# Dropping the row norms of queries and keys, and moving the low-part subtraction of the attention weights from GpSimd to VectorE

## The chip, the cores and the metric

The kernel runs on one core of one Trainium2 chip. The metric is the time of one execution in device microseconds. Before the change three runs gave 878.05, 881.35 and 883.31 us; their median, 881.35 us, is the time before.

## The reference

Inputs: q, k, v of 2 batches x 8 heads x 768 tokens x 64; 16 centroids of 64 for each head; two feed-forward layers of 512 -> 2048 -> 512, whose weights come as float64; and alpha (2048).

```
q_n = q / (norm(q) + 1e-6);  k_n, c_n likewise
q_assign = argmax over clusters of q_n . c_n;  k_assign likewise
scores = where(q_assign == k_assign, q k^T / 8, -1e9)
attn = softmax(scores);  x = attn v           # 1536 tokens x 512
h = x w1_in;  x = (h * sigmoid(h)) w1_out
h = x w2_in;  x = (max(h,0) + alpha * min(h,0)) w2_out
```

A token's own norm scales all 16 of its similarities by the same positive factor. The position of the largest one does not depend on it (ties by rounding apart).

## The kernel before

Every float32 operand of a matrix product is scaled by a power of two and split into two fp16 parts, high and low; three products (high-high, high-low, low-high) are summed in PSUM. The split of something takes two steps: a copy to fp16 (the high part) and a subtraction that leaves the low part.

A **unit** is one head of one tile of 128 tokens; there are 12 tiles x 8 heads = 96 units. For a unit, `front` issues:

- on TensorE the scores, 128 x 768, in two banks of PSUM (L482 the cluster mask, L486 the product itself);
- on VectorE the largest score of a row (L498, over 768), then the scale (L501) and the bias (L502) of the exponential, one number a row each;
- on ScalarE the exponential (L504) and its fp16 copy, the high part (L511);
- the subtraction that makes the low part (L513), on VectorE for the 12 units that `P_LO_DVE` names and on GpSimd for the other 84;
- on SyncE's queue the transposing DMA of both parts (L519), from one of two buffers `hl` that the units use in turn.

Two units later `back` multiplies the transposed weights with the values (L531). `attention` is a generator over the units. Between them it prepares keys and values of a head pair (`prep_k_0`, `prep_k_a`, `prep_k_b`, `prep_v`) and the queries of the next tile (`prep_q_a`, `prep_q_b`). These find each row's cluster: `one_hot` scales the similarities by the inverse row norm (L276), finds the largest (L277), compares (L278) and so on. The inverse norms come from `reduce_sum` over the squares (L335 for keys, L435 for queries) and from `inv_norm`: a power on GpSimd (L296; at the start a square root on ScalarE, L294), an add (L297) and a reciprocal (L298), both on VectorE.

The weights come in pieces of 1 MB. A piece is turned from float64 to float32 by `to_f32` (ScalarE L596 and L600, or GpSimd L604 for the scaling; VectorE L607 and L610 put the bits together) and split by `split` (GpSimd L617 and VectorE L618, or other mixes). The first layer runs in seven chunks of one or two tiles (`layer1`: L858 and L889 on TensorE, L864 and L868 on ScalarE, L865 and L869 on VectorE), with the units dealt out between its steps (`UNITS_BY_CHUNK`). The second layer (L961, L992) follows, with its own weights prepared before and beside it.

What stands here is the order of issue in the program. The framework's scheduler then sets the order on each engine, from its own model of times. Each engine takes its instructions in that order; semaphores between the engines are set by the framework. GpSimd and VectorE work beside each other. A buffer's next writer waits for its last reader.

Of the kernel before, what the change touches and what calls it, by code (L numbers as in the profile page):

```python
# [9 lines left out]
F32 = mybir.dt.float32  # L10
# [4 lines left out]
ACTF = mybir.ActivationFunctionType  # L15
# [3 lines left out]
# Token tiles per chunk of the first layer: (first, number).  # L19
CHUNKS = ((0, 1), (1, 1), (2, 2), (4, 2), (6, 2), (8, 2), (10, 2))  # L20
# The order of issue. A unit is one head of one token tile; "by chunk" says how far the
# units are to be issued by the end of a chunk of the first layer.
# [11 lines left out]
# Which engine does what: "a" ScalarE, "p" GpSimd (by batch and head pair, or by weight and  # L34
# piece; SPLIT has the modes of split()); the units whose low parts VectorE makes.
# [4 lines left out]
P_LO_DVE = (33, 35, 37, 39, 57, 59, 61, 63, 65, 67, 69, 71)  # L40
# [6 lines left out]
def cluster_attention_silu_prelu(  # L47
# [13 lines left out]
    """Cluster-masked attention, then a SiLU and a PReLU feed-forward layer.  # L61

    Every float32 operand of a product is scaled by a power of two (found on the
    chip from a norm, so that nothing overflows) and split into fp16 parts
    hi + lo; hi*hi + hi*lo + lo*hi accumulate in float32.
    Token 6p+t of a batch sits on partition p of tile t.
    """
    nc = tc.nc
# [88 lines left out]
    def pow2_scale(ss_ps, n, top, smax, s_out, inv_out):  # L157
        """s = 2^e with sqrt(ss) * s <= 2^top (and s <= 2^smax); inv = 1/s."""
        u = scr(n).bitcast(I32)
        nc.vector.tensor_scalar(u, ss_ps.bitcast(I32), 24, None, op0=ALU.logical_shift_right)  # L160
        if smax is not None:
            nc.vector.tensor_scalar(u, u, float(max(0, 62 + top - smax)), None, op0=ALU.max)
        e = 189 + top
        nc.vector.tensor_scalar(
            s_out.bitcast(I32), u, float(-e), -BIT23, op0=ALU.add, op1=ALU.mult
        )
        nc.vector.tensor_scalar(
            inv_out.bitcast(I32), u, float(254 - e), BIT23, op0=ALU.add, op1=ALU.mult
        )
# [13 lines left out]
    def psum(kind, *dims):  # L183
        """A bank of PSUM: of the scores', of preparations, of weight norms and layers, or
        (once the preparations are over) any of the last two for layers."""
# [20 lines left out]
    def all_sum(cols, kind="m"):  # L206
        """Sum over partitions (and over the given [128, n] groups), on every partition."""
        n = cols[0].shape[1]
        ps = psum(kind, n)
        for i, c in enumerate(cols):  # L210
            nc.tensor.matmul(out=ps, lhsT=ones, rhs=c, start=(i == 0), stop=(i == len(cols) - 1))
        return ps

    def bc(a, n):
        return a.unsqueeze(2).to_broadcast([128, a.shape[1], n])

    def issue_after(later, earlier):
        """Keep two instructions of one engine in order."""
# [51 lines left out]
    def one_hot(sims, rn, n, w2, o, a, b):  # L270
        """w2[:, :, 64:80] = a * (cluster is the first of the highest sims) + b."""
        x = view(o, F32, n, C)
# [3 lines left out]
        nc.vector.tensor_tensor(out=x, in0=sims, in1=bc(rn, C), op=ALU.mult)  # L276
        nc.vector.reduce_max(out=m, in_=x, axis=AX.X)  # L277
        nc.vector.tensor_tensor(out=y, in0=x, in1=bc(m, C), op=ALU.is_equal)  # L278
# [8 lines left out]
    rn_cols = {H: col(2 * H), 2 * T: col(NP * 2 * T)}  # L287

    def inv_norm(ss, n, early=False):
        """1 / (sqrt(ss) + 1e-6)"""  # L290
        r = rn_cols[n]
        r = r[:, n * ring(f"rn{n}", r.shape[1] // n):][:, :n]
        if early:
            nc.scalar.activation(out=r, in_=ss, func=ACTF.Sqrt)  # L294
        else:
            nc.gpsimd.tensor_tensor(out=r, in0=ss, in1=half[:, 0:n], op=ALU.pow)  # L296
        nc.vector.tensor_scalar(r, r, 1e-6, None, op0=ALU.add)  # L297
        nc.vector.reciprocal(out=r, in_=r)  # L298
        return r

# [20 lines left out]
    def scaled(raw, ss, top, smax, inv, eng, kind):  # L321
        """raw *= s, the power of two that brings the norm under 2^top."""
# [7 lines left out]
    def prep_k_0(b, pr):  # L330
        kr = view(kv_raw(b, pr)[0], F32, G, D)
        sq = view(k_pre(b, pr), F32, G, D)
        ssk, ss = scr(G), scr(1)
        nc.scalar.activation(out=sq, in_=kr, func=ACTF.Square, accum_out=ss)
        nc.vector.reduce_sum(out=ssk, in_=sq, axis=AX.X)  # L335
# [6 lines left out]
        kv_state[b, pr] = inv_norm(ssk, G, b == 0)  # L342
# [42 lines left out]
    def v_scales(b):  # L385
        """No row of the attention output has a larger norm than sqrt(8 m), where m is the
        largest sum of squares of a pair's values in one partition."""
# [8 lines left out]
    def prep_k_b(b, pr):  # L396
        rn = kv_state.pop((b, pr))
# [11 lines left out]
        one_hot(sims, rn, G, w2, k_pre(b, pr), -MASK, 0.0)  # L409
# [14 lines left out]
    q_state = {}  # L424

    def prep_q_a(n):
        raw = view(o_qraw, F32, H, 2, D)[:, :, n % 2, :]
        sq = view(o_preq, F32, H, D)
        ssq = scr(H)
# [5 lines left out]
        nc.vector.reduce_sum(out=ssq, in_=sq, axis=AX.X)  # L435
# [10 lines left out]
        q_state[n] = inv_norm(ssq, H, n == 0)  # L446

    def prep_q_b(n):
        rn = q_state.pop(n)
# [9 lines left out]
        one_hot(sims, rn, H, w2, o_preq, -MASK, MASK)  # L459
# [12 lines left out]
    def front(u):  # L472
# [29 lines left out]
        nc.vector.tensor_tensor(out=bias, in0=nm, in1=scl, op=ALU.mult)  # L502
# [41 lines left out]
    def x_done(n):  # L544
        """Normalise the tile's attention output, split it and transpose the parts."""
# [23 lines left out]
    # float64 bits come in as pairs of 32-bit words. A piece is 1024 elements per partition:  # L569
    # 256 columns of w_in, or two row tiles of w_out.  # L570
# [19 lines left out]
    def to_f32(raw, out, meng):  # L590
        """float64 to float32 by bits: sign, low 8 bits of the exponent's excess over
        2^-127, 20 + 3 bits of the mantissa. The scale by 2^-112 drops the exponent's
        excess range (what lies below 2^-119 stays below it); the last 3 bits come from
        the low word, rounded without a carry (and exactly where float32 is exact)."""
# [43 lines left out]
    def in_tasks(w, raws, o_dst, kind, modes, mp):  # L638
        """Tasks that convert, scale (per piece) and split w_in; and its scales."""
# [41 lines left out]
    def out_tasks(w, raws, o_ts, o_dst, m_in, kind, modes, mp):  # L681
        """The same for w_out: one scale, that also evens out the scales of w_in's pieces."""
# [60 lines left out]
    def attention():  # L743
# [26 lines left out]
        nc.scalar.activation(out=scr(1), in_=kv_state[0, NP - 1][:, 0:1], func=ACTF.Exp)  # L770
# [10 lines left out]
        for u in range(NU + LAG):  # L781
# [11 lines left out]
            # key / value preparation  # L793
# [22 lines left out]
            # query preparation of the next tile  # L816
# [273 lines left out]
```

## Time and profile before

| what | value |
|---|---|
| runs, us | 878.05, 881.35, 883.31 (median 881.35) |
| span of the profiled execution, us | 887.3 (the only time shown of it) |
| TensorE matmul busy | 712.1 us, 80% of the span |
| VectorE (DVE) busy | 627.4 us, 71% |
| ScalarE (ACT) busy | 468.4 us, 53% |
| GpSimd (POOL) busy | 319.1 us, 36% |
| granted TensorE clock, mean | 0.922 |

The shares are averages over very different stages. Up to about 22 us the first loads and preparations run. Up to about 200 us the first layer's weights are prepared beside the first 28 units. Up to about 520 us the other 68 units run, dealt out between the steps of the first layer. Then come the rest of the first layer, the second layer's weights, and from 618 us the second layer itself.

### The profile page before, as it was taken

The page shows a single profiled execution, that of the slowest core. Times are in us where ns is not written, and L with a number is a line of the kernel's source. Part 1 is how long each engine was busy: PE and PEld are TensorE (multiplying, and loading weights), DVE is VectorE, ACT ScalarE, POOL GpSimd, SP SyncE. Part 2 cuts the span into 40 slices and gives each one's busy share as a digit, 9 for nine tenths or more (in the row PEclk, how much of TensorE's full clock was granted, in tenths as well). Part 3 has the DMA queues.
Part 4 walks back from the last instruction along what each step waited for, and adds up shares of the span by engine and source line. Part 5 has one row for each costly group of instructions (what it writes and reads, how often), then busy time and mean ns, then how long its engine had stood idle before and what let it go on. Part 6 is the DMA issues. An engine that isn't in the chain of part 4 may idle for free.

```text
span 887.3 us, 16339 instructions
## 1 busy us (share of the span) xinstructions
PE 712.1 (80%) x6484; PEld 492.5 (56%) x6484; DVE 627.4 (71%) x1298; ACT 468.4 (53%) x866; POOL 319.1 (36%) x216
## 2 busy tenths in 40 slices
PE   1444376766898887789988988879968999999998
PEld 1222255656776776578766767768433444444443
DVE  7999998987869777865986589596895048306700
ACT  7845577736678564565765676878461013102200
POOL 4757764694434652231354432332191000000000
PEclk9995566789899998989999999999998999999999
DMA  8979788657798677486778694455100000000000
GB/s 245 247 204 223 208 221 172 108 120 120 128 153 143 123 150 123 70 145 120 113 108 140 109 242 137 143 189 192 48 1 4 32 13 1 13 24 12 1 24 24
DMA packets 241596, 101.86 MB, mean 115 GB/s; under 512 B 217328, under 2 KB 227568, under 8 KB 241392
## 3 DMA queue, kind: packets, MB, share of 16 engines
q1 hardware_dynamic: 241520, 100.83, 52.8%
q8 instruction: 50, 0.82, 0.4%
q14 instruction: 26, 0.21, 0.1%
HBM read 44.08 MB, written 3.15 MB: 53 GB/s over the span
## 4 chain that ended last, share of the span: by engine, by line
PE 34%; DVE 25%; DMA 17%; POOL 10%; ACT 8%; issue 6%; SPq 1%; POOLq 0%; ACTq 0%; DVEq 0%
DMA arena<-arena 12%; PE w L992 9%; PE w L961 6%; PE m L992 5%; PE m L961 4%; POOL arena L513 4%; PE w L858 4%; DVE arena L607 3%; DMA arena<-in_moe_w_out_dram 2%; DVE arena L869 2%; DVE stat L498 2%; DVE arena L610 2%; PE w L889 2%; ACT arena L511 2%; PE x L531 2%
## 5 line engine op out<-in xcount | busy, mean ns | idle before, releaser
L513 POOL TENSOR_TENSOR arena<-arena 128x768 f16<-128x768 f32 x84 | 147.5, 1763 | 186.7 <-ACT arena L511 184.4
L858 PE MATMUL w<-arena 128*128 128x256 f16 (+1 forms) x1212 | 142.6, 276 | 30.2 <-DVE arena L865 27.7
L858 PEld LDWEIGHTS <-arena 128*128 128x128 f16 x1344 | 127.1, 107 | 56.0 <-issue 37.7
L889 PEld LDWEIGHTS <-arena 128*128 128x128 f16 x1344 | 121.1, 102 | 19.0 <-issue 2.5
L889 PE MATMUL w<-arena 128*128 128x256 f16 (+1 forms) x1200 | 126.1, 264 | 3.2 <-DVE arena L618 1.2
L504 ACT ACTIVATE arena<-s,stat 128x768 f32<-128x768 f32 x96 | 94.5, 985 | 57.0 <-DVE stat L502 42.5
L498 DVE TENSOR_REDUCE stat<-s 128x1 f32<-128x768 f32 x96 | 91.0, 950 | 39.4 <-PE s L486 39.0
L961 PEld LDWEIGHTS <-arena 128*128 128x128 f16 x576 | 57.1, 100 | 80.3 <-issue 15.9
L531 PE MATMUL x<-arena 128*128 128x64 f16 x1728 | 74.9, 203 | 32.0 <-DMA arena<-arena 31.9
L482 PE MATMUL s<-arena 80*128 80x384 f16 x192 | 71.2, 371 | 35.8 <-ACT arena L504 29.7
L511 ACT ACTIVATE arena<-arena 128x768 f16<-128x768 f32 x96 | 80.1, 840 | 32.3 <-DMA arena<-arena 32.2
L992 PEld LDWEIGHTS <-arena 128*128 128x128 f16 x576 | 56.4, 98 | 67.9
L531 PEld LDWEIGHTS <-arena 128*128 128x128 f16 x1728 | 68.9, 105 | 44.6 <-DMA arena<-arena 39.8
L961 PE MATMUL w<-arena 128*128 128x512 f16 x384 | 87.6, 383 | 5.8 <-DVE arena L971 5.8
L992 PE MATMUL w<-arena 128*128 128x512 f16 x384 | 83.9, 379 | 0.0
L974 ACT ACTIVATE arena<-arena,stat 128x512 f16<-128x512 f32 x48 | 34.5, 720 | 88.2 <-DVE arena L971 86.2
L486 PE MATMUL s<-arena 128*128 128x384 f16 x192 | 71.7, 374 | 0.0
L869 DVE SCALAR_TENSOR_TENSOR arena<-arena 128x256 f16<-128x256 f32 (+1 forms) x112 | 62.4, 564 | 5.9 <-ACT arena L868 5.8
L604 POOL TENSOR_SCALAR arena<-arena 128x1024 f32<-128x1024 f32 x28 | 40.6, 1452 | 57.8 <-DMA arena<-in_moe_w_out_dram 32.5
L607 DVE SCALAR_TENSOR_TENSOR arena<-arena 128x1024 int32<-128x1024 int32 x32 | 45.1, 1408 | 20.3 <-ACT arena L600 10.7
L864 ACT ACTIVATE arena<-w,stat 128x256 f32<-128x256 f32 (+1 forms) x101 | 43.3, 432 | 27.9 <-PE w L858 19.4
L970 DVE TENSOR_SCALAR arena<-w,stat 128x512 f32<-128x512 f32 x32 | 23.9, 748 | 46.9 <-PE w L961 46.5
(145 smaller groups left out, 1133.9 us busy)
## 6 DMA issues: line engine op xcount, KB each, us to landing
arena<-in_moe_w_in_dram SPq DMA_DIRECT2D x16, 1024.0 KB, 6.3
arena<-in_moe_w_out_dram SPq DMA_DIRECT2D x16, 1024.0 KB, 5.4
arena<-in_k_dram SPq DMA_DIRECT2D x8, 384.0 KB, 4.3
arena<-in_q_dram SPq DMA_DIRECT2D x6, 512.0 KB, 5.3
arena<-in_v_dram SPq DMA_DIRECT2D x8, 384.0 KB, 5.5
out_dram<-arena SPq DMA_DIRECT2D x12, 256.0 KB, 2.0
arena<-arena SPq DMA_TRANSPOSE x149, 4.0
arena<-in_moe_alpha_dram SPq DMA_DIRECT2D x1, 1024.0 KB, 6.5
```

Of the source, the lines that this page charges most:

```text
L486: nc.tensor.matmul(out=sc[:, j, :hs], lhsT=qt1[:, h], rhs=kt1[:, h % 2, j * hs:(j + 1) * hs], start=False, stop=True,)
L498: nc.vector.tensor_reduce(out=nm, in_=sc[:, :, :hs], axis=AX.XY, op=ALU.max, negate=True)
L504: nc.scalar.activation(out=view(o, F32, 2, hs), in_=sc[:, :, :hs], func=ACTF.Exp, scale=scl, bias=bias, accum_out=sums[n % 2][:, h:h + 1],)
L511: nc.scalar.activation(out=hl[:, 0], in_=p, func=ACTF.Copy)
L513: en.tensor_tensor(out=hl[:, 1], in0=p, in1=hl[:, 0], op=ALU.subtract)
L531: nc.tensor.matmul(out=x_ps[0][:, h], lhsT=pt[:, ph * T + t], rhs=vt[:, h % 2, t, vh], start=(i == 0), stop=(i == 3 * T - 1),)
L607: nc.vector.scalar_tensor_tensor(out=lo, in0=hi, scalar=3, in1=lo, op0=ALU.logical_shift_left, op1=ALU.bitwise_or)
L858: nc.tensor.matmul(out=hp, lhsT=wi[:, a, kd, f % 2 * 128:f % 2 * 128 + 128], rhs=mov(bb, kd), start=(i == 0), stop=(i == 3 * KD - 1),)
L869: nc.vector.scalar_tensor_tensor(out=g[:, f, 1], in0=th, scalar=2.0 ** -16, in1=g[:, f, 0], op0=ALU.mult, op1=ALU.subtract,)
L889: nc.tensor.matmul(out=acc, lhsT=wo[:, a, f % 2, dt * 128:(dt + 1) * 128], rhs=g[:, f, bb], start=(i == 0), stop=(i == 3 * KF - 1),)
L961: nc.tensor.matmul(out=hp, lhsT=in_piece(o_a + 24 * KB, f // 2)[:, a, kd, f % 2 * 128:][:, :128], rhs=x[bb][:, kd], start=(i == 0), stop=( ...
L992: nc.tensor.matmul(out=acc, lhsT=g[:, f, a, t * 128:(t + 1) * 128], rhs=out_piece(o_w, f // 2)[:, bb, f % 2], start=(i == 0), stop=(i == 3 ...
```

## The change

Three edits, besides comments:

1. The row norms go. `inv_norm` and the sums over squares for it are no longer there; `one_hot` looks for the largest similarity in PSUM directly, without the multiplication by the inverse norm. The sum of squares of the whole operand, from which the power of two is found, stays.
2. The bias of the exponential (L502) is made by `tensor_scalar` with one number a row as scalar, in place of `tensor_tensor`.
3. `P_LO_DVE` names all 96 units: each low-part subtraction of the attention weights (L513) is on VectorE.

```diff
-P_LO_DVE = (33, 35, 37, 39, 57, 59, 61, 63, 65, 67, 69, 71)
+P_LO_DVE = range(96)
...
-    def one_hot(sims, rn, n, w2, o, a, b):
+    def one_hot(sims, n, w2, o, a, b):
-        x = view(o, F32, n, C)
         y = view(o + KB, F16, n, C)
         z = view(o, F16, n, C)
         m = scr(n)
-        nc.vector.tensor_tensor(out=x, in0=sims, in1=bc(rn, C), op=ALU.mult)
-        nc.vector.reduce_max(out=m, in_=x, axis=AX.X)
-        nc.vector.tensor_tensor(out=y, in0=x, in1=bc(m, C), op=ALU.is_equal)
+        nc.vector.reduce_max(out=m, in_=sims, axis=AX.X)
+        nc.vector.tensor_tensor(out=y, in0=sims, in1=bc(m, C), op=ALU.is_equal)
...
-    def inv_norm(ss, n, early=False):
-        """1 / (sqrt(ss) + 1e-6)"""
-        r = rn_cols[n]
-        r = r[:, n * ring(f"rn{n}", r.shape[1] // n):][:, :n]
-        if early:
-            nc.scalar.activation(out=r, in_=ss, func=ACTF.Sqrt)
-        else:
-            nc.gpsimd.tensor_tensor(out=r, in0=ss, in1=half[:, 0:n], op=ALU.pow)
-        nc.vector.tensor_scalar(r, r, 1e-6, None, op0=ALU.add)
-        nc.vector.reciprocal(out=r, in_=r)
-        return r
...
-        nc.vector.reduce_sum(out=ssk, in_=sq, axis=AX.X)
...
-        kv_state[b, pr] = inv_norm(ssk, G, b == 0)
...
-        nc.vector.reduce_sum(out=ssq, in_=sq, axis=AX.X)
...
-        q_state[n] = inv_norm(ssq, H, n == 0)
...
-        nc.vector.tensor_tensor(out=bias, in0=nm, in1=scl, op=ALU.mult)
+        nc.vector.tensor_scalar(bias, nm, scl, None, op0=ALU.mult)
...
-        nc.scalar.activation(out=scr(1), in_=kv_state[0, NP - 1][:, 0:1], func=ACTF.Exp)
+        nc.scalar.activation(out=scr(1), in_=isk[0][:, NP - 1:NP], func=ACTF.Exp)
```

The program is shorter, so the line numbers of the changed kernel are smaller: L498, L501, L502 and L513 are L474, L477, L478 and L489 there; L604 and L617 are L580 and L593; L380 is L363; L607, L610 and L618 are L583, L586 and L594.

On **GpSimd**, while the first layer's weights are prepared, subtractions of units (L513) and powers of the norms (L296) stand between the conversions (L604) and splits (L617) of weights before the change:

```order
L380 TENSOR_TENSOR arena<-arena 128x12x64
L513 TENSOR_TENSOR arena<-arena 128x768 x2
L617 TENSOR_SCALAR arena<-arena,stat 128x1024
L604 TENSOR_SCALAR arena<-arena 128x1024
L617 TENSOR_SCALAR arena<-arena,stat 128x1024
L513 TENSOR_TENSOR arena<-arena 128x768 x2
L604 TENSOR_SCALAR arena<-arena 128x1024 x2
L617 TENSOR_SCALAR arena<-arena,stat 128x1024
L513 TENSOR_TENSOR arena<-arena 128x768 x2
L296 TENSOR_TENSOR stat<-stat,half 128x8
```

The same place of GpSimd in the changed kernel, after the low parts of the values (L363):

```order
L363 TENSOR_TENSOR arena<-arena 128x12x64
L593 TENSOR_SCALAR arena<-arena,stat 128x1024
L580 TENSOR_SCALAR arena<-arena 128x1024
L593 TENSOR_SCALAR arena<-arena,stat 128x1024
L580 TENSOR_SCALAR arena<-arena 128x1024 x2
L593 TENSOR_SCALAR arena<-arena,stat 128x1024
```

The weights' instructions keep their order among themselves, and nothing of a unit stands between them.

On **VectorE** near the last units of the attention, before the change, the maximum (L498), scale (L501) and bias (L502) of a unit stand close together, with the last steps of a tile (L557, L560, L561) between them (s with a number is a unit's scores):

```order
L498 TENSOR_REDUCE stat_75<-s_5999 128x1
L557 TENSOR_TENSOR arena_73<-x_5522,stat_75 128x512
L501 TENSOR_SCALAR stat_75<-stat_75 128x1
L498 TENSOR_REDUCE stat_75<-s_6041 128x1
L560 CAST arena_73<-arena_73 128x512
L502 TENSOR_TENSOR stat_75<-stat_75 128x1
```

There, after the change, the subtraction of one unit (L489) stands between the scale (L477) and the bias (L478) of the next:

```order
L474 TENSOR_REDUCE stat_75<-s_5942 128x1
L477 TENSOR_SCALAR stat_75<-stat_75 128x1
L489 TENSOR_TENSOR arena_73<-arena_73 128x768
L478 TENSOR_SCALAR stat_75<-stat_75 128x1
L474 TENSOR_REDUCE stat_75<-s_6008 128x1
```

VectorE now reaches the bias of a unit only past the subtraction of the unit before it. While the weights are prepared, VectorE's order after the change has pieces of weights (L583, L586) and the norm-free steps of `one_hot` (L283, L284) between the bias of a unit (the first L478) and the next subtraction:

```order
L478 TENSOR_SCALAR stat<-stat 128x1
L283 TENSOR_TENSOR arena<-arena,stat 128x128
L583 SCALAR_TENSOR_TENSOR arena<-arena 128x1024
L586 SCALAR_TENSOR_TENSOR arena<-arena 128x1024
L478 TENSOR_SCALAR stat<-stat 128x1
L284 TENSOR_SCALAR arena<-arena 128x8x16
L160 TENSOR_SCALAR stat<-w 128x1
L586 SCALAR_TENSOR_TENSOR arena<-arena 128x1024
L489 TENSOR_TENSOR arena<-arena 128x768
```

Other work thus stands between what ScalarE needs from VectorE for a unit and what VectorE needs back from it.

## Rows read from the trace of the kernel before

**Rows 1.** Busy time of each engine by stage (the columns are named first).
```profile
core 0: us, PE busy (x) PEld busy (x) DVE busy (x) ACT busy (x) POOL busy (x), PEclk, DMA share, GB/s
22.00:200.00 178.00, 96.69 (x1090) 75.59 (x1091) 169.26 (x343) 111.23 (x201) 120.11 (x72) 0.76 0.80 187
200.00:520.00 320.00, 271.58 (x3406) 224.59 (x3403) 240.65 (x599) 201.94 (x409) 130.39 (x80) 0.95 0.75 127
```

**Rows 2.** Groups of VectorE, 22 to 200 us: count | busy us, mean ns | idle before.
```profile
L607 DVE SCALAR_TENSOR_TENSOR arena<-arena 128x1024 int32<-128x1024 int32 x15 | 23.5, 1569 | 0.9 <-POOL arena L604 0.6 <-ACT arena L596 0.3
L610 DVE SCALAR_TENSOR_TENSOR arena<-arena 128x1024 int32<-128x1024 int32 x15 | 22.9, 1534 | 0.0
L618 DVE SCALAR_TENSOR_TENSOR arena<-arena,stat 128x1024 f16<-128x1024 f32 x14 | 22.8, 1631 | 0.0
L502 DVE TENSOR_TENSOR stat<-stat 128x1 f32<-128x1 f32 x27 | 12.4, 461 | 0.0
...
L297 DVE TENSOR_SCALAR stat<-stat 128x8 f32<-128x8 f32 (+1 forms) x6 | 3.4, 564 | 0.7 <-POOL stat L296 0.5
L435 DVE TENSOR_REDUCE stat<-arena 128x8 f32<-128x512 f32 x5 | 3.4, 674 | 0.0
...
L335 DVE TENSOR_REDUCE stat<-arena 128x12 f32<-128x768 f32 x3 | 2.8, 927 | 0.0
...
L276 DVE TENSOR_TENSOR arena<-m,stat 128x128 f32<-128x128 f32 (+1 forms) x8 | 2.4, 301 | 0.0
```

**Rows 3.** Groups of GpSimd, 22 to 200 us.
```profile
L513 POOL TENSOR_TENSOR arena<-arena 128x768 f16<-128x768 f32 x25 | 47.7, 1914 | 24.9 <-ACT arena L511 23.6 <-issue 1.3
...
L296 POOL TENSOR_TENSOR stat<-stat,half 128x8 f32<-128x8 f32 (+1 forms) x7 | 13.8, 1978 | 1.9 <-DVE stat L435 1.8 <-DVE stat L160 0.2
```

**Rows 4.** VectorE by line, whole span: shortest/median/longest ns, first and last start.
```profile
L502 DVE TENSOR_TENSOR stat<-stat x96: 101/153/1652, 39.8 to 522.7; 128x1 f32<-128x1 f32 x96
L501 DVE TENSOR_SCALAR stat<-stat x96: 196/203/215, 37.2 to 522.5; 128x1 f32<-128x1 f32 x96
L513 DVE TENSOR_TENSOR arena<-arena x12: 943/958/1372, 241.0 to 435.7; 128x768 f16<-128x768 f32 x12
L607 DVE SCALAR_TENSOR_TENSOR arena<-arena x32: 1161/1225/2653, 14.6 to 633.9; 128x1024 int32<-128x1024 int32 x32
L610 DVE SCALAR_TENSOR_TENSOR arena<-arena x32: 1207/1216/2661, 16.6 to 636.4; 128x1024 int32<-128x1024 int32 x32
L618 DVE SCALAR_TENSOR_TENSOR arena<-arena,stat x20: 1269/1523/2816, 27.0 to 650.8; 128x1024 f16<-128x1024 f32 x20
L869 DVE SCALAR_TENSOR_TENSOR arena<-arena x112: 273/414/1862, 123.8 to 601.2; 128x256 f16<-128x256 f32 x80, 128x128 f16<-128x128 f32 x32
L551 DVE TENSOR_SCALAR stat<-stat x12: 156/172/2609, 86.9 to 528.6; 128x8 f32<-128x8 f32 x12
```

**Rows 5.** Timeline, two instructions at 464.8 us: start, duration, engine, line.
```profile
464.80 1.64 POOL L513 TENSOR_TENSOR arena<-arena 128x768 f16<-128x768 f32 x1 [2.38 <-ACT arena L511]
...
464.90 1.56 DVE L502 TENSOR_TENSOR stat<-stat 128x1 f32<-128x1 f32 x1
```

**Rows 6.** Groups of VectorE, 200 to 520 us, and of GpSimd last.
```profile
L869 DVE SCALAR_TENSOR_TENSOR arena<-arena 128x256 f16<-128x256 f32 (+1 forms) x70 | 40.1, 580 | 2.8 <-ACT arena L868 2.7
...
L502 DVE TENSOR_TENSOR stat<-stat 128x1 f32<-128x1 f32 x67 | 24.7, 370 | 0.8
...
L513 DVE TENSOR_TENSOR arena<-arena 128x768 f16<-128x768 f32 x12 | 12.2, 1019 | 8.3 <-ACT arena L511 8.2
...
L513 POOL TENSOR_TENSOR arena<-arena 128x768 f16<-128x768 f32 x58 | 97.9, 1696 | 157.0 <-ACT arena L511 156.0 <-POOL arena L326 0.5 <-POOL arena L513 0.2
```

**Rows 7.** Shares of the chain that ended last, 200 to 520 us, by line.
```profile
by line: DMA arena<-arena 27.6%; PE w L858 7.9%; PE w L889 5.7%; POOL arena L513 5.6%; issue 4.8%; DVE stat L498 4.1%; DVE arena L869 4.0%; ACT arena L511 3.9%; PE x L531 3.4%; PE s L486 2.3%; PE s L482 2.3%; DVE arena L865 2.0%; DMA arena<
```

**Rows 8.** Pieces of that chain at 302 us: start, length, what.
```profile
302.17 1.66 POOL stat L296
...
303.85 1.60 DVE stat L297
```

More of the change, by code (lines that the diff above doesn't have):

```diff
@@ L285, in one_hot @@
         nc.vector.tensor_scalar(w2[:, :, D:D + C], y, a, b, op0=ALU.mult, op1=ALU.add)
-    rn_cols = {H: col(2 * H), 2 * T: col(NP * 2 * T)}
-    def inv_norm(ss, n, early=False):
-        r = rn_cols[n]
-        r = r[:, n * ring(f"rn{n}", r.shape[1] // n):][:, :n]
-        if early:
-            nc.scalar.activation(out=r, in_=ss, func=ACTF.Sqrt)
-        else:
-            nc.gpsimd.tensor_tensor(out=r, in0=ss, in1=half[:, 0:n], op=ALU.pow)
-        nc.vector.tensor_scalar(r, r, 1e-6, None, op0=ALU.add)
-        nc.vector.reciprocal(out=r, in_=r)
-        return r
     G = 2 * T
@@ L332, in prep_k_0 @@
         sq = view(k_pre(b, pr), F32, G, D)
-        ssk, ss = scr(G), scr(1)
+        ss = scr(1)
         nc.scalar.activation(out=sq, in_=kr, func=ACTF.Square, accum_out=ss)
-        nc.vector.reduce_sum(out=ssk, in_=sq, axis=AX.X)
         if b == 0 and pr == 0:
@@ L396, in prep_k_b @@
     def prep_k_b(b, pr):
-        rn = kv_state.pop((b, pr))
         did.add(("k", b, pr))
@@ L408, in prep_k_b @@
                 )
-        one_hot(sims, rn, G, w2, k_pre(b, pr), -MASK, 0.0)
+        one_hot(sims, G, w2, k_pre(b, pr), -MASK, 0.0)
         k_t2[b, pr] = nc.sync.dma_start_transpose(
@@ L422, in load_q @@
         )
-    q_state = {}
     def prep_q_a(n):
@@ L428, in prep_q_a @@
         sq = view(o_preq, F32, H, D)
-        ssq = scr(H)
         ss = scr(1)
@@ L445, in prep_q_a @@
         nc.vector.tensor_copy(out=w2[:, :, 0:D], in_=w1[:, :, 0:D])
-        q_state[n] = inv_norm(ssq, H, n == 0)
     def prep_q_b(n):
-        rn = q_state.pop(n)
         qt1 = view(o_qt + 4 * KB * (n % 2), F16, H, 128)
@@ L458, in prep_q_b @@
                 )
-        one_hot(sims, rn, H, w2, o_preq, -MASK, MASK)
+        one_hot(sims, H, w2, o_preq, -MASK, MASK)
         q_t2[n] = nc.sync.dma_start_transpose(
```

## The prediction

> **What bounds the kernel now.** I read the busy time by stage first. From 22 to 200 us VectorE is busy 169.3 of 178 us, while TensorE is busy 96.7 and GpSimd 120.1 [rows 1]: that stage is VectorE's. From 200 to 520 us no engine is full. TensorE is busy 271.6 of 320 us and VectorE 240.7; DMA stands at 0.75 [rows 1]. There I read the chain that ended last. Its largest part is transposing DMA, 27.6%, which can't start before a unit's low part is made; the subtraction on GpSimd is 5.6% by itself [rows 7]. The last unit's bias is made at 522.7 us [rows 4]. After that nothing that the change edits runs, apart from single subtractions at the end; the second layer's weights and the second layer take the rest. So a gain has to be made before about 520 us, and the rest follows earlier by the same amount.
>
> The third view is the duration of one instruction by line. The bias (L502) works on one number a row and takes 153 ns in the median, but up to 1652 [rows 4]. The timeline shows why: at 464.90 us it starts 0.10 us behind a subtraction on GpSimd (464.80, 1.64 us long) and ends with it, at 466.46 against 466.44 [rows 5]. The same stretching shows in L607, L610, L618 and L869, whose longest is over twice their shortest [rows 4]; each of them reads two tensors. L501 reads one and a scalar: 196 to 215 ns in all 96 cases [rows 4]. So part of VectorE's busy time is waiting for GpSimd, and the 84 subtractions there do much of that harm. This is the heart of my argument: they cost VectorE time although they don't run on it.
>
> **The change part by part, 22 to 200 us.** VectorE is full here, so I sum its busy time and let the sum reach the end whole.
>
> *Norms.* L435, L335, L276 and L297 take 3.4 + 2.8 + 2.4 + 3.4 us [rows 2]: 12.0 us go. The seven powers on GpSimd, 13.8 us [rows 3], go with them.
>
> *Bias.* 27 of them take 12.4 us [rows 2]. The new form was not run. Its nearest row is L501, also one number a row with a pointer scalar: 203 ns [rows 4]. 27 x 0.203 = 5.5, so 6.9 us go. Bounds: at the present median (153 ns, no wait) 8.3; if the new form waits for GpSimd like the old one, 0.
>
> *Other waits.* Against their shortest times, L607 loses 15 x (1.569 - 1.161) = 6.1 us, L610 15 x (1.534 - 1.207) = 4.9 and L618 14 x (1.631 - 1.269) = 5.1 [rows 2, 4], 16.1 together. Subtractions and powers are 61.5 of GpSimd's 120.1 us [rows 1, 3], and at 1.9 us each they are longer to wait for than the rest. I choose 60%: 9.7 us go. Bounds: 0 (the weights' own instructions move into the gaps) and 16.1.
>
> *Added.* 25 subtractions leave GpSimd in this stage [rows 3]. On VectorE one takes 958 ns in the median, 943 to 1372 [rows 4]: 24.0 us come, between 23.6 and 34.3.
>
> Sum: -12.0 - 6.9 - 9.7 + 24.0 = -4.6 us, say **-5**. Both ends: -12.0 - 8.3 - 16.1 + 23.6 = -13, and -12.0 + 34.3 = +22.
>
> **200 to 520 us.** VectorE has 79 us of idle time here [rows 1], so its sum decides nothing; the chain does.
>
> *Subtraction.* 5.6% of 320 us is 17.9 us of the chain [rows 7]. 1696 ns on GpSimd [rows 6] become 958 on VectorE [rows 4]: 17.9 x (1 - 0.958 / 1.696) = **-7.8**. Ends: 0 (VectorE comes to it late) and -7.8.
>
> *Bias.* 67 take 24.7 us [rows 6]; at 203 ns they would take 13.6, so 11.1 us go. The exponential waits for each, but only some of these stand on the chain: I take half, **-5.5**, between 0 and -11.1.
>
> *Low parts of the first layer.* 70 of L869 take 40.1 us [rows 6]; at the median of 414 ns [rows 4] 29.0, so 28% of its time is waiting. It is 4.0% of the chain, 12.8 us [rows 7]. Subtractions are 97.9 of GpSimd's 130.4 us [rows 1, 6]. 12.8 x 0.28 x 0.75 = **-2.7**; ends 0 and -3.6.
>
> *Norms.* At 302 us the preparation of the second batch's keys stands on the chain with a power on GpSimd (1.66 us) and the add behind it (1.60) [rows 8]: **-3**. Ends 0 and -5, if another tile's norms matter too.
>
> *The new wait.* A subtraction on VectorE holds what is queued behind it until ScalarE has made the high part. The 12 that are there now cost 8.3 us of idle time, 0.69 each [rows 6]; 58 more at this rate are 40 us. Idle time costs only where late work is behind it. In the order of the changed kernel other work stands before most subtractions; in the last 20 or so units the bias of the next unit stands right behind. 20 x 0.15 us = **+3**, between 0 and 40.
>
> SyncE issues the same transposes, each up to 0.7 us earlier; fewer GpSimd instructions stand before the weights' own. The edit of the table load costs nothing: it only names another column.
>
> Here the Trainium skill speaks against one term. The row first: eight numbers a row through the same operation (L551) take 172 ns in the median but up to 2609, while L501 with one number never waits [rows 4]. The skill (SBUF — State Buffer, Who interferes with whom) says that `tensor_scalar` on VectorE can use both ports to SBUF and is then shut out by GpSimd until the other's end. Read broadly, this would leave the new bias waiting for the weights' instructions. The measurement of L501 decides for me: the bias terms stand at -6.9 and -5.5; taken like L551 they would be 0, and the sum smaller by 12.4.
>
> **Sum:** -5 - 7.8 - 5.5 - 2.7 - 3 + 3 = -21 us. The profiled execution's span is 887.3 us, 0.7% over the median of the runs, 881.35; nothing else of its time is shown. 866.3 / 887.3 x 881.35 = 860.5. I forecast **860 us**.
>
> **The rivals.**
>
> *VectorE's queue becomes the chain (slower).* The place is L513 in front of the next unit's bias. For it: 0.69 us of idle time per subtraction there now [rows 6], and a stage that is already 95% full. 25 + 58 subtractions x 0.69 = 57 us. Without my +3 the gains are 24 us, so it decides once over 24 of the 57 reach the end. With three quarters, 43, the time is 887.3 - 24 + 43 = 906, or 900 us against the median; with half, 28.5, about 886. Against it: the order puts weights' work between. The Trainium skill (TensorE: Matmul & The Clock Gate, in the part on the array's sub-arrays) says that VectorE takes its queue strictly in order. By that rule nothing overtakes a held subtraction, and the idle time before L513 agrees.
>
> *DMA takes the gain (no change).* The transposes are the largest part of the chain [rows 7], and DMA stands at 0.80 from 22 to 200 us [rows 1]. If low parts made earlier only queue longer, the chain's -7.8, -5.5 and -2.7 are lost: 887.3 - 5 = 882, or 877 us. Against it: from 200 us on the share is 0.75, so there is room.
>
> *The waits go almost whole (larger gain).* Five more lines with two inputs in the first stage are not priced above. With the ends of all terms: -13 - 7.8 - 11.1 - 3.6 - 5 = -40, or 841 us; with the unpriced waits some 835.
>
> *The bias still waits* like L551: 860 + 12 = 872 us.
>
> **How the numbers follow.** Forecast (848 to 868) 0.45; the bias still waits (869 to 876) 0.08; larger gain (below 848) 0.18; DMA takes it 0.12; VectorE's queue 0.17. About 0.5% is what a measurement of this kernel can tell from no change, 877 to 886 us. Faster 0.45 + 0.08 + 0.18 = 0.71; same 0.12; slower 0.17. The range for 8 in 10 goes from 836, near the unpriced end of the larger gain, to 888, just past half of the queue's waits reaching the end.
>
> **What would show it.** The bias at about 0.2 us with no long cases; L607, L610 and L618 nearer 1.2 to 1.3 us; the subtraction at 0.95 to 1.05 us on VectorE; VectorE's busy time about even or lower although it has 84 more instructions; the last unit near 500 us instead of 523; and the stretch from there to the end as long as before. I would be wrong if VectorE sits idle before L513 for 40 us or more and TensorE waits for its transposes longer than now, if the bias still shows cases over 1 us, or if the last unit comes earlier and the end doesn't.

## The result and the profile after

After the change four runs gave a median of 872.88 us (869.46 to 873.64), beside 880.17 us (878.05 to 883.31) for the kernel before, whose three runs have been joined by a fourth. The ratio is 0.9881, with a 95% interval of 0.9846 to 0.9917: faster by 1.2%, some 10.5 us. The two medians alone differ by 7.3 us (0.9917), at the upper end of that interval. The forecast was 860 us, faster, with a range of 836 to 888. The sign was right and the time lies in the range; the gain is half of the 21 us that the sum gave.

The profiled execution after took 873.64 us itself, and its span is 871.5 us. In the profiled executions of all kernels here some 2 us lie around the span. The span of before, 887.3 us, therefore belongs to an execution of about 889 us, some 8 us above its median: of the 15.8 us between the two spans only about 10 are the change, and what follows goes by ratios wherever it speaks of a gain.

Busy time by stage, after (the columns of [rows 1]):

```profile
22.00:200.00 178.00, 100.99 (x1175) 80.13 (x1176) 161.95 (x348) 115.01 (x208) 66.13 (x39) 0.75 0.85 189
200.00:520.00 320.00, 271.80 (x3424) 224.41 (x3424) 244.27 (x626) 209.87 (x422) 21.32 (x15) 0.97 0.76 134
```

GpSimd's busy time fell from 120.1 to 66.1 and from 130.4 to 21.3 us. VectorE took over 84 subtractions and yet is busy 7.3 us less in the first stage and only 3.6 more in the second. Over the whole span it is 607.4 us after 627.4. Norms and bias are in these figures too; edit 3 alone, in TensorE's old order, has 627.1 us (the table further down). The heart of the argument, that subtractions on GpSimd cost VectorE nearly what they take on it, holds.

VectorE by line, after (the view of [rows 4]):

```profile
L478 DVE TENSOR_SCALAR stat<-stat x96: 164/207/215, 35.0 to 513.0; 128x1 f32<-128x1 f32 x96
L489 DVE TENSOR_TENSOR arena<-arena x96: 939/954/2875, 45.4 to 523.2; 128x768 f16<-128x768 f32 x96
L583 DVE SCALAR_TENSOR_TENSOR arena<-arena x32: 1209/1217/2198, 14.4 to 618.1; 128x1024 int32<-128x1024 int32 x32
L594 DVE SCALAR_TENSOR_TENSOR arena<-arena,stat x20: 1269/1280/2134, 23.4 to 634.9; 128x1024 f16<-128x1024 f32 x20
```

The bias never waits (215 ns at most). The subtraction takes 954 ns in the median, but up to 2875: it reads two tensors itself, and now it is the one that waits for GpSimd's weights (four of the 96 take over 1.2 us, each beside a scaling or split of weights there). L594 is at 1280 ns in the median instead of 1523. The last bias comes at 513.0 us instead of 522.7 [rows 4], and from there to the end it takes 358.5 us instead of 364.6. Some 8 us of these differences are the longer execution before, so this pair can't show where the gain is made.

Groups of VectorE, 22 to 200 us, after (the view of [rows 2]):

```profile
L489 DVE TENSOR_TENSOR arena<-arena 128x768 f16<-128x768 f32 x27 | 29.3, 1085 | 4.2 <-ACT arena L487 4.2
...
L594 DVE SCALAR_TENSOR_TENSOR arena<-arena,stat 128x1024 f16<-128x1024 f32 x14 | 21.6, 1547 | 0.0
L586 DVE SCALAR_TENSOR_TENSOR arena<-arena 128x1024 int32<-128x1024 int32 x15 | 21.3, 1422 | 0.0
L583 DVE SCALAR_TENSOR_TENSOR arena<-arena 128x1024 int32<-128x1024 int32 x15 | 21.2, 1416 | 0.0
...
L478 DVE TENSOR_SCALAR stat<-stat 128x1 f32<-128x1 f32 x28 | 5.7, 204 | 0.1
```

Shares of the chain that ended last, 200 to 520 us, by line, after (the view of [rows 7]):

```profile
by line: DMA arena<-arena 22.3%; PE w L865 9.3%; PE w L834 8.6%; PE x L507 5.1%; PE s L458 3.3%; PE s L462 3.2%; DMA arena<-in_moe_w_in_dram 2.5%; issue 2.2%; DVE arena L489 2.0%; DVE stat L474 1.7%; DMA arena<-in_v_dram 1.4%; ACT arena L48
```

The subtraction's share went from 5.6% on GpSimd to 2.0% on VectorE, and the low parts of the first layer (4.0% before) are no longer among the first lines. In their place TensorE's own work stands on the chain: the first layer (L834, L865) and the value products (L507) have 23.0% where they had 17.0.

The waits of TensorE and VectorE, whole span: what waited for what, us in total, times, longest. The kernel before first, then the changed one:

```profile
PE x L531 <- DMA arena<-arena: 31.9, 27, 3.5
PE s L482 <- ACT arena L504: 29.7, 15, 5.5
```

```profile
PE x L507 <- DMA arena<-arena: 78.9, 48, 8.0
PE s L458 <- ACT arena L480: 6.2, 6, 3.8
DVE arena L489 <- ACT arena L487: 32.0, 30, 3.4
```

VectorE sits idle 32.0 us before the subtraction (8.2 before the change), under the 40 that the prediction named as a warning. But TensorE waits 78.9 us for the transposed weights of its value products where it waited 31.9. That was the other half of the warning, and the search began there.

### The profile page after: what moved, and what is told of

It reads as the page before. It is cut to its first block, busy times and chain, and to the rows that moved or that the text cites. A ratio compares the mean times of both kernels' runs of the same rounds, so it can differ in the third digit from the quotient of the medians.

```text
span 871.5 us, 16209 instructions
## 1 busy us (share of the span) xinstructions
PE 704.7 (81%) x6484; PEld 487.1 (56%) x6484; DVE 607.4 (70%) x1302; ACT 468.5 (54%) x861; POOL 153.5 (18%) x117
## 4 chain that ended last, share of the span: by engine, by line
PE 36%; DMA 12%; DVE 10%; ACT 4%; issue 2%; POOL 1%; SPq 0%; POOLq 0%; DVEq 0%; ACTq 0%
PE w L968 10%; DMA arena<-arena 8%; PE w L937 6%; PE m L968 5%; PE m L937 4%; PE w L865 3%; PE w L834 3%; DMA arena<-in_moe_w_out_dram 2%; PE x L507 2%; DMA arena<-in_moe_w_in_dram 2%; DVE arena L583 1%; DVE arena L586 1%; PE s L458 1%; PE s L462 1%; DVE arena L951 1%
## 5 line engine op out<-in xcount | busy, mean ns | idle before, releaser
L834 PEld LDWEIGHTS <-arena 128*128 128x128 f16 x1344 | 126.6, 107 | 35.1 <-issue 18.8
L834 PE MATMUL w<-arena 128*128 128x256 f16 (+1 forms) x1212 | 137.5, 273 | 10.6 <-DVE arena L841 8.5
L507 PE MATMUL x<-arena 128*128 128x64 f16 x1728 | 75.0, 202 | 79.9 <-DMA arena<-arena 78.9
L865 PEld LDWEIGHTS <-arena 128*128 128x128 f16 x1344 | 118.5, 100 | 20.7 <-POOL arena L605 2.9
L865 PE MATMUL w<-arena 128*128 128x256 f16 (+1 forms) x1200 | 123.9, 260 | 5.4 <-POOL arena L605 2.5
L507 PEld LDWEIGHTS <-arena 128*128 128x128 f16 x1728 | 66.2, 104 | 95.4 <-DMA arena<-arena 91.8
L489 DVE TENSOR_TENSOR arena<-arena 128x768 f16<-128x768 f32 x96 | 95.0, 991 | 32.3 <-ACT arena L487 32.0
L474 DVE TENSOR_REDUCE stat<-s 128x1 f32<-128x768 f32 x96 | 91.1, 951 | 28.4 <-PE s L462 28.2
L937 PEld LDWEIGHTS <-arena 128*128 128x128 f16 x576 | 57.0, 99 | 80.0 <-issue 15.5
L968 PEld LDWEIGHTS <-arena 128*128 128x128 f16 x576 | 56.4, 98 | 68.0
L580 POOL TENSOR_SCALAR arena<-arena 128x1024 f32<-128x1024 f32 x28 | 43.2, 1541 | 287.2 <-DMA arena<-in_moe_w_in_dram 219.1
L458 PE MATMUL s<-arena 80*128 80x384 f16 x192 | 69.8, 364 | 17.6 <-DMA arena<-arena 11.1
L462 PE MATMUL s<-arena 128*128 128x384 f16 x192 | 69.8, 364 | 0.0
L840 ACT ACTIVATE arena<-w,stat 128x256 f32<-128x256 f32 (+1 forms) x101 | 43.5, 434 | 29.3 <-PE w L834 24.2
L583 DVE SCALAR_TENSOR_TENSOR arena<-arena 128x1024 int32<-128x1024 int32 x32 | 42.9, 1340 | 22.1 <-ACT arena L572 8.3
L845 DVE SCALAR_TENSOR_TENSOR arena<-arena 128x256 f16<-128x256 f32 (+1 forms) x112 | 49.7, 451 | 6.0 <-ACT arena L844 5.9
```

The costliest lines, as they stand in the source:

```text
L458: nc.tensor.matmul(out=sc[:, j, :hs], lhsT=qt2[0:D + C, h], rhs=kt2[0:D + C, h % 2, j * hs:(j + 1) * hs], start=True, stop=False,)
L462: nc.tensor.matmul(out=sc[:, j, :hs], lhsT=qt1[:, h], rhs=kt1[:, h % 2, j * hs:(j + 1) * hs], start=False, stop=True,)
L474: nc.vector.tensor_reduce(out=nm, in_=sc[:, :, :hs], axis=AX.XY, op=ALU.max, negate=True)
L489: en.tensor_tensor(out=hl[:, 1], in0=p, in1=hl[:, 0], op=ALU.subtract)
L507: nc.tensor.matmul(out=x_ps[0][:, h], lhsT=pt[:, ph * T + t], rhs=vt[:, h % 2, t, vh], start=(i == 0), stop=(i == 3 * T - 1),)
L583: nc.vector.scalar_tensor_tensor(out=lo, in0=hi, scalar=3, in1=lo, op0=ALU.logical_shift_left, op1=ALU.bitwise_or)
```

## The experiments

Each kernel ran beside the kernel before on the same chip; the three groups (four kernels each) ran on three chips, and only ratios are compared between them. Edits are numbered as in the section on the change: 1 the row norms, 2 the bias, 3 the subtractions.

### One edit at a time

Edit 1 alone takes the norms out of the kernel before, as in the diff above. Edit 2 alone is

```diff
-        nc.vector.tensor_tensor(out=bias, in0=nm, in1=scl, op=ALU.mult)
+        nc.vector.tensor_scalar(bias, nm, scl, None, op0=ALU.mult)
```

and edit 3 alone

```diff
-P_LO_DVE = (33, 35, 37, 39, 57, 59, 61, 63, 65, 67, 69, 71)
+P_LO_DVE = range(96)
```

Edit 1, expected: 

> The kernel before without the row norms (edit 1 alone); subtractions and bias as before. By the terms of the prediction the norms are worth 12 us of VectorE's time up to 200 us and 3 us of the chain later; as a part of the sum that would be about -10 us, so 870 against 880 before. Rival (the norms were hidden, since VectorE's freed time is taken by waits for GpSimd's subtractions, which all stay): 878 to 882.

Edit 3, expected: 

> The kernel before with all 96 subtractions on VectorE (edit 3 alone); norms and old bias stay. If the waits that GpSimd's subtractions cause are the heart of the matter, the 84 added subtractions (some 83 us on VectorE) are paid back by shorter waits: 872 to 878, bias (L502) without cases over 1 us apart from powers and weights. Rival (VectorE's full first stage and its queue decide): the added time comes out at the end, 885 to 900.

Edit 2, expected: 

> The kernel before with the bias made by tensor_scalar (edit 2 alone); GpSimd keeps its 84 subtractions. By the terms of the prediction -6.9 and -5.5 us: 868 to 872, all 96 cases of L502 near 0.2 us. Rival (the waits only move to the next instruction with two inputs, or were not on the chain): 877 to 882. Rival by L551: L502 still shows cases over 1 us and the time does not change.

Measured, as ratios to the kernel before: edit 1 0.9985 (0.996 to 1.0009), edit 3 1.0113 (1.0086 to 1.014), edit 2 1.0001 (0.998 to 1.0022). No edit alone gains anything measurable, and one loses: for each it was a rival that came true. Together they gave 0.9881. With edit 2 alone the bias on VectorE reads, by line:

```profile
L502 DVE TENSOR_SCALAR stat<-stat x96: 155/202/216, 39.6 to 516.3; 128x1 f32<-128x1 f32 x96
L551 DVE TENSOR_SCALAR stat<-stat x12: 156/163/1477, 91.2 to 519.6; 128x8 f32<-128x8 f32 x12
```

So the new form does what it was to do even with 84 subtractions on GpSimd. VectorE is busy 611.1 us instead of 627.4 for it, and the time doesn't move. What edit 3 alone lost shows in TensorE's waits of that kernel:

```profile
PE x L531 <- DMA arena<-arena: 76.3, 47, 6.7
```

That is the wait of the changed kernel (78.9 us), without the other two edits.

### TensorE's order

The framework's scheduler sets the order on every engine anew after each edit, TensorE's too. How many other units' scores stand on TensorE between a unit is scores and its value product, counted in the traces and averaged over units 0 to 27, 28 to 63 and 64 to 95:

```
before         3.9  3.4  2.9
after          3.1  2.9  2.5
edit 3 alone   3.0  2.6  2.5
```

Edit 3 by itself draws the value products nearer to their scores (edit 1 by itself doesn't: 4.2, 3.4, 3.2). As I read it, the scheduler's model of times counts on the shorter subtraction; its model was not looked into. Where the transposing DMA lands later than that, TensorE stands still. To try this, TensorE's instructions were held in a written order, everything else left to the scheduler (cut; the list begins like this for the order of the kernel before):

```diff
+PE_ORDER = [(0, 4), (5, 40), (82, 1), (4, 1), (45, 2), (53, 24), (47, 2), (129, 1), (77, 1), (49, 4), (78, 4), (105, 24)
...
-                nc.tensor.matmul(
+                mms.append(nc.tensor.matmul(
...
+    pe = [i for a, n in PE_ORDER for i in range(a, a + n)]
+    for a, b in zip(pe, pe[1:]):
+        issue_after(mms[b], mms[a])
```

The kernel before, with TensorE in the order of the changed kernel: 

> The kernel before, with TensorE's order held to that of the changed kernel; the scheduler still sets the other engines' order. Theory (the engine moves change little by themselves; the scheduler's new order on TensorE makes the gain): 870 to 876. Rival (the gain is VectorE's, freed of waits; the order is worth nothing): 879 to 885, or more, since that order expects low parts earlier than GpSimd makes them.

All edits, with TensorE in the order of the kernel before: 

> The changed kernel with TensorE's order held to that of the kernel before. Theory (order makes the gain): 879 to 885. Rival (freed VectorE makes it): 868 to 875, as the changed kernel.

Edit 3 alone, in the order of the changed kernel: 

> Edit 3 alone (all subtractions on VectorE, norms and old bias stay), with TensorE's order held to that of the changed kernel. Alone it took 1.0113 of before, with units 89 to 95 placed behind first-layer steps on TensorE. Theory (that order was the loss): 872 to 879. Rival (the added 83 us on VectorE are the loss whatever the order): 889 to 894.

Measured: 1.0409 (1.0381 to 1.0438), 0.982 (0.9796 to 0.9843) and 1.0155 (1.0131 to 1.018). The theories of all three failed (919.4, 867.1 and 896.4 us), and the third lies above its rival's range too. The order of the changed kernel isn't where the gain comes from. It costs the kernel before 4.1%, and with all edits it gives 0.9881 where the old order gives 0.982. Holding TensorE's order moves the other engines' orders too: between the changed kernel and all edits in the old order some 920 of VectorE's 1302 instructions keep their sequence, counted by line and shape. "Order" means here TensorE's, with what the scheduler made of the others beside it. TensorE's waits for transposes follow it: 85.6 us for the kernel before in the new order, and for all edits in the old order:

```profile
PE s L461 <- ACT arena L483: 31.6, 16, 5.3
PE x L510 <- DMA arena<-arena: 18.2, 13, 5.3
```

The 78.9 us became 18.2, while TensorE's wait for the exponential (which reads a unit is scores out of their bank) came back from 6.2 to 31.6. So most of the 60 us are exchanged for other waits, and the two kernels differ by some 5 us of time. Edit 3 alone in the order of the changed kernel was no better than in its own; I took this for a sign that order had no part in that loss. That reading fell with the last group of runs.

### VectorE's load in the last third

From the first maximum of unit 64 to that of unit 95 took 124 us before and 133 us after, while the units before them had become faster. Two kernels tried VectorE as the reason: one leaves the subtractions of units 64 to 95 to GpSimd (`P_LO_DVE = range(64)`), one makes each subtraction stand behind the bias of the next unit, with its transpose issued after it (cut; `low_part` issues the subtraction that is held and then its transpose):

```diff
-        en = nc.vector if u in P_LO_DVE else nc.gpsimd
-        en.tensor_tensor(out=hl[:, 1], in0=p, in1=hl[:, 0], op=ALU.subtract)
...
+        low_part(bias_i)
+        held.append((u, p, hl))
```

The first: 

> The changed kernel with the subtractions of units 64 to 95 back on GpSimd. Theory (in the last third the subtraction stands before the next unit's bias in VectorE's queue, and that cost 9 us: units 64 to 96 take 133 us after and 124 before): units 64 to 96 take about 124 us again, 863 to 866. Rival (transposes or the order on TensorE slow that stretch, not VectorE's queue): 131 to 135 us there and 871 to 875. Rival (contention): GpSimd's 32 subtractions lengthen VectorE's two-input instructions again, time over 875.

The second: 

> The changed kernel with each subtraction issued behind the next unit's bias on VectorE, and its transpose after it. If the bias behind the subtraction cost the last third 9 us: 862 to 867, and the exponential of units 64 to 95 starts under 2.5 us after their maximum (2.93 in the changed kernel). Rival (that wait is hidden, and a later subtraction only makes the transposes late): 872 to 885, TensorE waits longer for its transposes.

Measured: 0.9851 (0.9811 to 0.9891) and 0.9898 (0.987 to 0.9926), beside 0.9881 (0.9846 to 0.9917) for the change itself. Neither differs from it beyond the intervals. The first did what it was to: in units 64 to 95 the bias starts 1.16 us behind the end of the maximum instead of 2.05, and the stretch takes 128 us, between the two cases expected. The second did not: its bias starts 2.04 us behind. In 13 of these 32 units (17 in the changed kernel) a subtraction still stands between maximum and bias, now that of the unit two before; VectorE's idle time before the subtraction fell to 24.4 us. So only the first bears on the slower rival, a held subtraction in front of the next bias: taking it away gained nothing beyond the intervals.

### Pairs of edits in one order

Since the order alone can move the time by 4%, the last four kernels all have TensorE in the order of the kernel before.

Edit 3: 

> The kernel before with all 96 subtractions on VectorE (edit 3 alone), TensorE's instructions held in the order of the kernel before; norms and old bias stay. Theory (once the subtractions are VectorE's, VectorE sets the pace, and only what relieves it makes the move pay): with none of the relief the ratio to the kernel before is 1.000 to 1.015, as with the scheduler's own order (1.011). Rival (the scheduler's order lost what the move alone gains): 0.985 to 0.995.

Edits 1 and 3: 

> Edits 1 and 3 (no norms, all subtractions on VectorE), the old two-tensor bias stays; TensorE's order is that of the kernel before. With edit 2 as well this order gave 0.982. Theory (each relief of VectorE counts for itself): norms take some 24 us of VectorE's work away, so most of the gain is here, 0.982 to 0.993; the bias is worth under 1% beside it. Rival (the bias alone carries the gain, since the exponential waits for it): 1.000 or more.

Edits 2 and 3: 

> Edits 2 and 3 (new bias, all subtractions on VectorE), the row norms stay on VectorE and GpSimd; TensorE's order is that of the kernel before. Theory (each relief of VectorE counts for itself): the bias saves little work once few subtractions are left on GpSimd, so the ratio is 0.995 to 1.010. Rival (the bias alone carries the gain): 0.982 to 0.990.

All edits, the last 32 subtractions on GpSimd: 

> All three edits, but the subtractions of units 64 to 95 stay on GpSimd; TensorE's order is that of the kernel before. If the last third's loss is VectorE's load, this adds to the 0.982 of the same order with all subtractions on VectorE: 0.970 to 0.980. If the loss was the order alone, the two don't add: 0.981 to 0.987.

Measured, with the kernel before itself ("none") and the kernel of the same order from above (0.982, of the second group). VectorE's busy time is that of the profile's first part:

| edits, all in TensorE's order of before | ratio to before (95%) | VectorE busy, us |
|---|---|---|
| none | 1 | 627.4 |
| 3 | 0.9985 (0.9961 to 1.0009) | 627.1 |
| 2 and 3 | 1.0041 (1.0023 to 1.006) | 629.2 |
| 1, 2 and 3 | 0.982 (0.9796 to 0.9843) | 602.6 |
| 1 and 3 | 0.9788 (0.9756 to 0.9821) | 600.9 |
| 1, 2 and 3, last 32 on GpSimd | 0.9769 (0.974 to 0.9797) | 589.4 |

Edit 3 alone neither gains nor loses in this order; in its own it lost 1.1%, in the changed kernel's 1.6%. So the order, as defined above, was that loss after all, and the kernel with the changed kernel's order couldn't show it, because that order costs as much. Edit 1 beside edit 3 brings 2% (0.9985 to 0.9788). Edit 2 beside edit 3 costs half a per cent (0.9985 to 1.0041); with edit 1 there as well the difference, 0.9788 to 0.982, lies within the intervals. The rival of these runs, that the bias carries the gain, is out. The theory that each relief of VectorE pays got the ranking right and the sizes a little wrong: edit 3 alone and edits 1 and 3 came out just below their ranges, and the bias was no relief. Why not shows in its rows, edit 3 alone and then edits 2 and 3:

```profile
L505 DVE TENSOR_TENSOR stat<-stat 128x1 f32<-128x1 f32 x96 | 18.3, 193 | 0.4
```

```profile
L505 DVE TENSOR_SCALAR stat<-stat 128x1 f32<-128x1 f32 x96 | 19.1, 204 | 0.5
```

With the subtractions gone from GpSimd the old bias takes 18.3 us for 96, where it took 38.1 before: its waits went with edit 3. The new form takes 19.1. It has nothing left to save.

VectorE by stage, edit 3 alone and then edits 1 and 3 (columns of [rows 1]):

```profile
22.00:200.00 178.00, 85.69 (x1002) 67.25 (x1003) 166.35 (x367) 112.24 (x200) 79.08 (x46) 0.76 0.81 187
200.00:520.00 320.00, 276.76 (x3513) 230.57 (x3511) 251.19 (x668) 209.61 (x421) 35.47 (x22) 0.95 0.75 133
```

```profile
22.00:200.00 178.00, 97.77 (x1135) 77.81 (x1136) 157.32 (x337) 113.65 (x203) 68.74 (x39) 0.84 0.80 187
200.00:520.00 320.00, 278.67 (x3552) 233.65 (x3550) 255.31 (x655) 217.33 (x437) 24.52 (x17) 0.96 0.78 143
```

Without the norms VectorE is busy 9.0 us less while the weights are prepared. The maximum of unit 28 starts at 204 instead of 211 us, that of unit 95 at 496 instead of 516, and from the last value product to the end it takes 350 instead of 347 us: all of the gain is made before the attention ends, as predicted. It grows on the way: 7.5 us at unit 28, 11.1 at unit 44, 15.3 at unit 56 and 20.7 at unit 95, so more than half of it comes after the weights of the first layer are prepared. Part of it shows in what the scores wait for: in edit 3 alone TensorE waits 21.0 us in 5 waits for transposing DMA before scores (10.7 at most), with edits 1 and 3 11.0 us in 3 (4.6 at most). All of these waits but one of 0.8 us are for the transposes behind the keys' `one_hot`. The last of them in the second batch lands at 336.1 us instead of 350.7. No run separates VectorE's relief from the shorter chain (power on GpSimd, add, reciprocal) in front of `one_hot`. The fuller second stage (255.3 against 251.2) is the same work done sooner.

The last kernel, 863.43 us (862.48 to 863.71), and edits 1 and 3 in the old order, 866.19 us (860.27 to 867.62), both beat the kernel before and the changed one. Their own intervals overlap. The last 32 subtractions on GpSimd add to the old order as the first case of that expectation had it (0.9769 after 0.982, with intervals that just touch): VectorE's load in the last third is worth some half a per cent, hardly clear of the noise.

Three things stay open. Edit 1 alone ran only in its own order, where value products stand further behind the scores than before (4.2, 3.4 and 3.2 units). It wasn't run in the order of the kernel before. So whether it needs edit 3 for its 2%, or needs only that order, is not known. And with kernels in their own orders VectorE's busy time does not foretell the time: edit 1 alone has 594.7 us and gains nothing. The agreement of the table is shown for one order of TensorE only. And VectorE's order was not held: between edit 3 alone and edits 1 and 3 in TensorE's old order, some 980 of the 1302 instructions that VectorE has left keep their sequence. How much of a step of the table is the edit is own and how much the scheduler's rearranging, no run shows.

## Why the prediction came out as it did

The change is faster, as forecast with a chance of 0.71, and its time is inside the range; the forecast itself was 13 us too low. The 872.88 us lie where the rival "the bias still waits" was put (869 to 876), but not for its reason: no bias waits. That agreement is luck.

**What bounds the kernel: right where one order of TensorE is held.** From edit 3 alone to edits 1 and 3 the gain is made before the attention ends. The changed kernel's last unit comes at 513 us and not near 500 (it does so with TensorE in the old order, 503). The stretch from the last value product to the end takes 338 to 350 us in all kernels, 348 before and 342 after; that spread is as large as the gain, so for the changed kernel itself "as long as before" is not shown.

**Norms, -12.0 and -3: right in the sum, beside edit 3.** There, in one order, they are worth 0.9788 / 0.9985, 2.0% or 17 us, against 15. The split was wrong: 7.5 us were there at unit 28, where 12 were forecast, and 13 came later, where 3 were. Alone, in their own order, they are worth 1 us, within the interval of 0.

**Bias, -6.9 and -5.5: right in VectorE's time, wrong in its worth; the step that failed.** The new price was right (207 ns against 203), and in the first stage 12.4 us became 5.7. But no run turns this into time. Edit 2 alone saves 16 us of VectorE's busy time and is worth 0. Edit 3 alone takes the bias's waits away as well, since it removes the subtractions for which it waits (38.1 us for 96 became 18.3); the prediction put them down to edit 2 alone. Beside it edit 2 has 18.3 - 19.1 = -0.8 us of VectorE's time left to save, and the runs show +0.6% beside edit 3 alone, and nothing beyond the intervals beside edits 1 and 3. In the first stage the saving was to reach the end whole, and later half of the biases were put on the path; neither shows in the end. Why half a per cent is lost beside edit 3, more than 0.8 us, isn't settled.

The Trainium skill, in "SBUF — State Buffer" (Who interferes with whom), lets `tensor_scalar` be shut out by GpSimd where it enters a mode that uses both ports. The trace with edit 2 alone draws the line inside that rule: 96 cases with one number a row end at 216 ns, 43 of them beside an instruction of GpSimd, while 12 with eight numbers go to 1477, and the three of these that ran beside one are the three longest. It is not the scalar taken from memory that keeps the bias clear, since an instruction with such a scalar and four numbers a row waits as well:

```profile
L492 DVE TENSOR_SCALAR stat<-stat x12: 215/220/1351, 30.7 to 456.8; 128x4 f32<-128x4 f32 x12
```

The Trainium skill's "VectorE: DVE Perf Modes" (Mode 2×_2P) has the mode split a row's elements into two halves, one for each port. The rows agree in so far as one number has no halves; that step is an inference. No run here shows the ports themselves.

**Edit 3's own terms, -9.7 + 24.0 - 7.8 - 2.7 + 3 = +7.** In the old order edit 3 alone is -0.15%, -1 us, within the intervals of 0. This looks 8 us better than forecast, but edit 3 as it ran also has the bias's relief, booked at -12.4 under edit 2. Edits 2 and 3 together were to bring 6.8 - 12.4 = -5.6 us; they brought 1.0041, +3.6 us. This is most of what the sum missed. Its pieces in the first stage: L583, L586 and L594 shed 15 x 0.153 + 15 x 0.112 + 14 x 0.084 = 5.2 us, not 9.7, because the weights' own instructions on GpSimd remain and meet them. The subtraction costs 27 x 1.085 = 29.3 us, not 25 x 0.958 = 24.0, in part for the same reason and in part because two more fall into the stage; 34 was the bound. The 0.15 us a unit of the new wait had no row behind it, and no run isolates it. The lines that the prediction left unpriced made up for this: L438, whose 6.7 us for 4 became 4.1 (L416 after), L869, L551 and the steps of `one_hot`.

**A term that is missing: TensorE's order, +5.** The prediction looked at the new order of VectorE and GpSimd, where instructions had moved engines, and not at TensorE's, where none had. There the scheduler drew each value product nearer to its scores. 0.9881 against 0.982 is 5.4 us of the 881, and TensorE's wait for transposes, 78.9 us, was the sign. The last third of the units is where it shows most: from unit 64 to unit 95 took 133 us with that order and 123 us with the old one (the stretch alone decides nothing, though: with edit 1 alone it is 142 us, at the time of the kernel before).

**The sum again**, in us of 881: edit 3 -1.3, edit 1 -17.4, edit 2 +2.8, the order +5.4, together -10.5. It is the ratio of 0.9881, since the four steps lead from one measured kernel to the next; each has an uncertainty of 2 to 4 us, and by the other way round, edits 2 and 3 first, they read +3.6 and then -19.5 for edit 1. The norms and edit 3 came out 2 and 8 us better than their terms, the bias 15 us worse and the order 5 us: that the time lies in the range owes something to errors that cancel.

**The rivals.** VectorE's queue as the chain: the idle time before the subtraction is there, 32.0 us, but leaving the last 32 subtractions to GpSimd gained nothing beyond the intervals in the changed kernel's order and some half a per cent in the old one. DMA taking the gain: a transpose takes 4.4 us before and after, from issue to landing, on average over units 64 to 95; over units 0 to 27 it is 5.1 us after 4.7, and again 4.7 with all edits in the old order (the time that the prediction gives this rival, 877 us, works out at 876). Waits going almost whole: VectorE's waits did go (its instructions lost some 125 us to overlap with GpSimd before and 50 after, each against the median of its kind without overlap), but VectorE's subtractions took 83 us in their place, so that only edit 1 was left as a net relief.

## What to carry to other kernels

When two edits cure the same wait, price the second only after the first: moving an engine's competing work away removes every wait for it, and a rewrite of the waiting instruction then has nothing left to save. After any change of an instruction's engine or length, compare the order on the engines that it doesn't touch, above all the one that is waited for; here the scheduler's new order of TensorE took back a third of the gain. Test single edits at a fixed order, of every engine if possible, or the order's own 1 to 4% will be read as theirs.

## What was not expected of the hardware

A `tensor_scalar` with one number a row on VectorE has no long cases beside GpSimd's subtractions (155 to 216 ns in 96, with edit 2 alone), while the same operation with eight numbers does (156 to 1477 in 12), and with four (215 to 1351 in 12). And the subtraction that was moved to VectorE to get out of the others' way is itself held up by what is left on GpSimd: 939 to 2875 ns, though only the weights, keys and values are still there; the longest four, from 1264 ns up, each run beside a scaling or split of weights.
